# Hash attention and a SwiGLU block on one core: from the sixth pair of heads on, q and k are turned by VectorE instead of TensorE

## The chip, the cores and the metric

The kernel runs on one NeuronCore of one Trainium2 chip. The metric is the time of one execution in microseconds (us) as the device reports it. Three runs of the kernel before gave 1186.89, 1187.71 and 1187.98 us; the median is 1187.71 us. The engines are named as in the profile: PE is TensorE, PEld its weight loads, DVE is VectorE, ACT is ScalarE, POOL is GpSimd, and SP is the engine whose queue issues most of the DMAs.

## The reference, cut to what matters

```python
# q, k, v: (4 batches, 8 heads, 768 positions, 64), proj: (64, 6), all float32
q_bits = (einsum('bhsd,dk->bhsk', q, proj) > 0)          # six sign bits per position
k_bits = (einsum('bhsd,dk->bhsk', k, proj) > 0)
mask   = q_bucket[:, :, :, None] == k_bucket[:, :, None, :]   # buckets: the bits as a number
scores = where(mask, q @ k.T / 8, -1e9)
attn   = softmax(scores)                                  # with 1e-9 added to the sum
a      = attn @ v                                         # (4, 8, 768, 64)
x      = a.transpose(0, 2, 1, 3).reshape(3072, 512)
out    = (silu(x @ w_gate) * (x @ w_val)) @ w_out         # w_gate, w_val: (512, 1536), w_out: (1536, 512)
```

The three weights are float64 on the host. The kernel narrows them to float32 itself.

## The kernel before

**Pairs.** Heads are worked on in pairs, 4 pairs per batch and 16 in all, numbered 0 to 15 (the "sixth pair" is number 5). A pair has 12 units: 2 halves of the queries by 6 chunks of 128 keys. The main loop takes two units per iteration, so a pair is six iterations, called iteration 0, 2, 4, 6, 8 and 10 below after the number of their first unit in the pair (the variable `at`).

**One iteration.** Every engine works strictly in the order in which the program was written; there is no scheduler. In each iteration the program writes, in this order: `score` for two units (PE multiplies, bits first and then q and k; ACT takes the exponential into a ring of four tiles `A`), `norm` where a half of a pair is complete (PE sums into tile `sum`, DVE takes the reciprocal `r`, then `e` and `xT`), `attend` for the two units of the iteration before (PE into `av`; DVE adds the exponentials up in `acc`), and then two steps, called `mine`, of the preparation of the next pair.

**The preparation of a pair** is `front(n)`. It is written during pair n-1. Heads lie in memory as position by feature, and PE needs feature by position. So `transpose` (L205) turns three 128 by 128 blocks with the identity matrix into a PSUM tile `tps`, and ACT copies them out into `qT` or `kT` (L208). That is done for q and k and two halves, four steps. Then come four steps of `hash_bits`: one multiplication by the hash weights into `hps` (L213), followed by ACT for q (`qb`, L216) or DVE for k (`kb`, L218). The eight steps fall on iterations 2, 4, 6 and 8, two in each. For all pairs but the first, `tps`, `hps` and `sum` share one single PSUM bank (`side_bank`); each must be read out before the next can be written. Pair 0 is prepared ahead of the loop and uses the two banks of `bank` in turn.

**The second part.** When the last half of a batch is normalised (iteration 2 of pairs 4, 8 and 12, and after pair 15), `push_ffn` appends 72 "atoms" of PE work for that batch: 48 `up` atoms (results `g` and `val`, L299, in the two banks of `bank`, read out by ACT with a tanh and by DVE into `t` and `ht`) and 24 `down` atoms (`po`, L320). From then on each iteration ends with about three atoms, and the steps of `mine` stand between them. In the first batch, pairs 0 to 3, there are no atoms, and PE has only attention to do.

**DVE's extra work.** `narrow` turns the weights into float32 in 36 pieces of seven DVE instructions (L162 to L178): two or three of them in an iteration without atoms, four behind each atom, until all pieces are done. POOL fetches the pieces (`words`).

**Fetching.** `load(n+2)` is written in iteration 10 of pair n: two DMAs each for q and k (192 KB each, 256-byte runs) and one for v, all on SP's queue, where the stores of `out` stand too.

Of the kernel before, what the change touches and what calls it, by code (L numbers as in the profile page):

```python
# [8 lines left out]
FP32 = mybir.dt.float32  # L9
# [8 lines left out]
def kernel(  # L18
# [17 lines left out]
    CH = NCH // 2  # L36
    HQ = CH * P
    NP = H // 2
    DM = H * D
# [39 lines left out]

    def load(n):  # L80
        b, pr = pairs[n]
        for name, src in (("q", q), ("k", k)):
            t = raw.tile([P, NCH, 2, D], FP32, tag=name + "raw", name=name + "raw")
            for h in range(2):
                nc.sync.dma_start(t[:, :, h, :],  # L85
                                  src[b, 2 * pr + h].rearrange("(p c) d -> p c d", c=NCH))
            raws[name, n] = t
        t = raw.tile([P, 2, NCH, D], FP32, tag="vraw", name="vraw")
        nc.sync.dma_start(
            t.rearrange("p h c d -> p h (c d)"),  # L90
            v[b, 2 * pr : 2 * pr + 2].rearrange("h (p c) d -> p h (c d)", c=NCH),
        )
        raws["v", n] = t

    load(0)

    hash_w = {}  # L100
    for name in "qk":
        hash_w[name] = konst.tile([P, P], FP32, tag="hash" + name, name="hash" + name)
        nc.vector.memset(hash_w[name], 0.0)
        for o in (0, D):
            for at in (0, NBITS) if name == "q" else (0,):
                nc.sync.dma_start(hash_w[name][o : o + D, o + at : o + at + NBITS], proj[:, :])

    def column(name, first, second, third, rest):
# [11 lines left out]
    times_k = column("times_k", OFF, -OFF / 2, -NBITS * OFF / 2, 0.0)  # L120
    ident = konst.tile([P, P], FP32, tag="ident", name="ident")
    make_identity(nc, ident)
    ones = konst.tile([P, D], FP32, tag="ones", name="ones")
    nc.vector.memset(ones, 1.0)


# [66 lines left out]
    T = {}  # L193
    bits = {}

    def front(n, bank=side_bank):


        def transpose(name, half):
            if half == 0:  # L200
                T[name, n] = opnd.tile([P, S], FP32, tag=name + "T", name=name + "T")
                bits[name, n] = opnd.tile([P, S], BF16, tag=name + "b", name=name + "b")
            ps = bank("tps")
            for i in range(CH):
                nc.tensor.transpose(ps[:, i * P : (i + 1) * P],  # L205
                                    raws[name, n][:, half * CH + i, :, :].rearrange("p h d -> p (h d)"),
                                    ident)
            nc.scalar.copy(T[name, n][:, half * HQ : (half + 1) * HQ], ps[:, 0:HQ])  # L208

        def hash_bits(name, half):  # L210
            cols = slice(half * HQ, (half + 1) * HQ)
            ps = bank("hps")
            nc.tensor.matmul(ps[:, 0:HQ], hash_w[name], T[name, n][:, cols], start=True, stop=True)  # L213
# [74 lines left out]

    atoms = []

    def push_ffn(b):
# [47 lines left out]

    for step in front(0, bank):  # L340
        step()
# [75 lines left out]
```

## Time and profile before

| what | value |
|---|---|
| median of three runs | 1187.71 us |
| the profiled execution's own time | 1187.64 us |
| its span on the core | 1185.9 us |
| outside the span | 1.7 us |
| PE, DVE, ACT busy | 98%, 43%, 24% |
| preparation of pair 0, ahead of the first score | 0 to 13.25 us |
| first batch (no atoms yet) | 13.25 to 143.37 us |
| pairs 4 to 15, attention with atoms between | 143.37 to about 1010 us |
| atoms alone | from about 1010 us to the end |

The profile comes from one execution whose time is within 0.1 us of the median. In rows of the timeline, the first number is the start in us, the second the time that the row covers, then engine, line, operation and "written tile <- read tiles". A row may cover several instructions (xN); each float32 product is recorded as two matmuls. What stands in square brackets is the time for which the engine sat idle before, and what ended that. In the chain of waits a piece is "start, length, engine and line". PE work is pipelined, so the recorded lengths of neighbours overlap: what a step costs is read from start to start.

### The profile page before, as it was taken

What the parts mean: (1) busy time and instruction counts of PE and PEld (TensorE: products, weight loads), DVE (VectorE), ACT (ScalarE), POOL (GpSimd) and SP (SyncE); (2) the same over time, 40 slices, a digit from 0 to 9 for tenths busy, and PEclk for the clock granted to TensorE, in tenths of its full rate; (3) what the DMA queues carried; (4) which work ended last, traced back from release to release, by engine and by line L of the source; (5) the groups of instructions that cost most, each with busy time, mean ns of one, the idle gap of its engine ahead of it and who ended that gap; (6) DMA issues with size and microseconds to landing.
All of it is one profiled execution on the core that took longest, in us unless ns stands there. A gap on an engine that the chain in (4) does not pass through costs nothing.

```text
span 1185.9 us, 10899 instructions
## 1 busy us (share of the span) xinstructions
PE 1156.9 (98%) x4480; PEld 573.2 (48%) x4480; DVE 508.2 (43%) x756; ACT 280.3 (24%) x441; POOL 19.2 (2%) x44
## 2 busy tenths in 40 slices
PE   7888899999999999999999999999999999999998
PEld 3333355555544445555554445555554444555543
DVE  3777689998852323343331233333233222222100
ACT  4444422222212222222221213222131211000000
POOL 0000000000000000000000000000000000000000
PEclk9999999999999999999999999999999999999999
DMA  5322222324210120100002012010000000000000
GB/s 142 76 76 76 58 79 92 101 71 113 88 40 18 37 57 1 40 1 1 14 1 58 18 36 49 1 40 1 14 1 1 18 18 18 1 1 0 1 27 27
DMA packets 63698, 44.76 MB, mean 38 GB/s; under 512 B 51872, under 2 KB 55968, under 8 KB 63648
## 3 DMA queue, kind: packets, MB, share of 16 engines
q1 hardware_dynamic: 58752, 26.23, 8.6%
q0 software_dynamic: 4896, 17.83, 4.9%
q8 instruction: 35, 0.57, 0.2%
q14 instruction: 15, 0.12, 0.0%
HBM read 37.76 MB, written 6.29 MB: 37 GB/s over the span
## 4 chain that ended last, share of the span: by engine, by line
PE 97%; DVE 2%; ACT 1%; DMA 0%; SPq 0%; issue 0%; ACTq 0%
PE val L299 21%; PE g L299 21%; PE po L320 21%; PE sc L244 14%; PE av L255 11%; PE hps L213 4%; PE sum L276 2%; PE tps L205 2%; DVE r L279 2%; ACT qb L216 0%; ACT qT L208 0%; DMA kraw<-in_k_dram 0%; SPq L85 0%; ACT A L246 0%; ACT o L324 0%
## 5 line engine op out<-in xcount | busy, mean ns | idle before, releaser
L299 PE MATMUL val<-xT,wv 128*128 128x384 f32 x768 | 266.2, 489 | 0.0
L299 PE MATMUL g<-xT,wg 128*128 128x384 f32 x768 | 265.9, 489 | 0.0
L320 PE MATMUL po<-wo,ht 128*128 128x512 f32 x576 | 257.1, 597 | 0.0
L246 ACT ACTIVATE A<-sc 128x768 f32<-128x768 f32 x192 | 155.5, 812 | 208.2 <-PE sc L244 177.0
L299 PEld LDWEIGHTS val<-xT,wv 128*128 128x128 f32 x768 | 142.5, 190 | 105.4 <-DVE acc L263 6.0
L299 PEld LDWEIGHTS g<-xT,wg 128*128 128x128 f32 x768 | 142.5, 190 | 105.1 <-DVE acc L263 6.0
L320 PEld LDWEIGHTS po<-wo,ht 128*128 128x128 f32 x576 | 106.8, 190 | 134.1 <-issue 130.7
L244 PE MATMUL sc<-qT,kT 64*128 64x384 f32 x768 | 156.0, 485 | 0.0
L279 DVE RECIPROCAL r<-sum 128x384 f32<-128x384 f32 x32 | 81.8, 2556 | 151.9 <-PE sum L276 151.9
L255 PE MATMUL av<-A,vraw 128*64 128x386 f32 x768 | 144.8, 498 | 0.0
L306 DVE SCALAR_TENSOR_TENSOR t<-t,g 128x384 f32<-128x384 f32 x96 | 53.1, 554 | 206.3 <-ACT t L305 206.3
L263 DVE TENSOR_TENSOR acc<-acc,A 128x768 f32<-128x768 f32 x128 | 122.3, 955 | 35.2 <-ACT A L246 30.3
L305 ACT ACTIVATE t<-g 128x384 f32<-128x384 f32 x96 | 47.1, 490 | 351.6 <-PE g L299 347.0
L311 DVE SCALAR_TENSOR_TENSOR ht<-t,val 128x384 f32<-128x384 f32 x96 | 53.1, 553 | 125.0 <-PE val L299 125.0
L255 PEld LDWEIGHTS av<-A,vraw 128*64 128x64 f32 x768 | 49.6, 137 | 82.4 <-issue 81.3
L244 PEld LDWEIGHTS sc<-qT,kT 64*128 64x128 f32 x768 | 69.0, 190 | 21.5 <-issue 21.5
L244 PE MATMUL sc<-qb,kb 64*128 64x384 bf16 x384 | 63.8, 329 | 0.1
L218 DVE TENSOR_SCALAR kb<-hps,above_k,times_k 128x384 bf16<-128x384 f32 x32 | 21.6, 675 | 83.9 <-PE hps L213 83.4
L244 PEld LDWEIGHTS <-kb 64*128 64x128 bf16 x384 | 18.7, 93 | 67.9 <-issue 55.1
L324 ACT COPY o<-po 128x512 f32<-128x512 f32 x24 | 14.0, 585 | 144.3 <-PE po L320 142.0
L216 ACT ACTIVATE qb<-hps,nudge 128x384 bf16<-128x384 f32 x32 | 18.6, 581 | 69.4 <-PE hps L213 69.3
L213 PE MATMUL hps<-qT,hashq 128*128 128x384 f32 x64 | 27.7, 515 | 5.5 <-DVE e L281 5.5
(58 smaller groups left out, 409.9 us busy)
## 6 DMA issues: line engine op xcount, KB each, us to landing
qraw<-in_q_dram SPq DMA_DIRECT2D x32, 192.0 KB, 3.7
kraw<-in_k_dram SPq DMA_DIRECT2D x32, 192.0 KB, 4.6
vraw<-in_v_dram SPq DMA_DIRECT2D x16, 384.0 KB, 3.4
words<-in_moe_w_val_dram POOLq DMA_DIRECT2D x12, 512.0 KB, 3.8
words<-in_moe_w_out_dram POOLq DMA_DIRECT2D x12, 512.0 KB, 3.6
out_dram<-o SPq DMA_DIRECT2D x24, 256.0 KB, 2.0
words<-in_moe_w_gate_dram POOLq DMA_DIRECT2D x10, 512.0 KB, 3.9
words<-in_moe_w_gate_dram SPq DMA_DIRECT2D x2, 512.0 KB, 5.8
```

The lines of the kernel that those rows point to most:

```text
L205: nc.tensor.transpose(ps[:, i * P : (i + 1) * P], raws[name, n][:, half * CH + i, :, :].rearrange("p h d -> p (h d)"), ident)
L213: nc.tensor.matmul(ps[:, 0:HQ], hash_w[name], T[name, n][:, cols], start=True, stop=True)
L244: nc.tensor.matmul(sc[:, h, 0:HQ], x["k", n][rows, ks], x["q", n][rows, qs], start=start, stop=not start)
L246: nc.scalar.activation(ring[u % RING][:, :, 0:HQ], sc[:, :, 0:HQ], AF.Exp, scale=SCALE)
L255: nc.tensor.matmul(ps[h * D : (h + 1) * D, 0:AW], raws["v", n][:, h, c, :], a[:, h, :], start=c == 0, stop=c == NCH - 1)
L263: nc.vector.tensor_tensor(acc[n, half], acc[n, half], a[:, :, 0:HQ], op=ALU.add)
L279: nc.vector.reciprocal(r, ps[:, 0:HQ])
L299: nc.tensor.matmul(ps[:, 0:HQ], w[:, j, f * P : (f + 1) * P], x[:, j, half * HQ : (half + 1) * HQ], start=j == 0, stop=j == NJ - 1)
L305: nc.scalar.activation(t, ps[:, 0:HQ], AF.Tanh, scale=0.5)
L306: nc.vector.scalar_tensor_tensor(out=t, in0=t, scalar=1.0, in1=ps[:, 0:HQ], op0=ALU.add, op1=ALU.mult)
L311: nc.vector.scalar_tensor_tensor(out=ht, in0=now["t"], scalar=0.5, in1=ps[:, 0:HQ], op0=ALU.mult, op1=ALU.mult)
L320: nc.tensor.matmul(ps, hs[half][f][:, i * P : (i + 1) * P], wo[:, f, :], start=f == 0, stop=f == NF - 1)
```

## The change

The change has three parts.

**Turning by DVE.** For pairs 5 to 15, q and k are fetched with four DMAs each instead of two. Each of them brings 32 features of one head to 32 partitions, 96 KB in runs of 128 bytes, such that every 32 by 32 block of the tile is still position by feature but stands where its turned block belongs. One DVE instruction for q and one for k (`nc.vector.transpose`, 128 by 768 float32) then turns all blocks in place of the four PE steps and the four ACT copies. `front` of these pairs has six steps, two of DVE in iteration 2, and the four of `hash_bits` in iterations 4 and 6.

**Banks of the first batch.** `front_bank` gives a step the single side bank if atoms are waiting. If none are, every third step (counted over all such steps) gets the side bank, and the other two get the banks of the atoms. This holds for the fronts of pairs 0 to 4.

**The start.** k of pair 0 goes on ACT's queue. The hash weights are fetched once per half (two DMAs on ACT's queue instead of six on SP's) and put in place by six small DVE copies. POOL instead of DVE clears their tiles. Nine multiplications of a tile of zeros stand at the head of PE.

PE in iterations 2 and 4 of pair 4, where the first atoms stand (`tps` and `hps` belong to the front of pair 5). Before:

```order
L276 MATMUL sum<-acc,ones 64x384 x2
L255 MATMUL av<-A,vraw 64x386 x4
L299 MATMUL g<-xT,wg 128x384 x4
L205 MATMUL tps<-ident,qraw 128x128 x3
L299 MATMUL val<-xT,wv 128x384 x4
L205 MATMUL tps<-ident,kraw 128x128 x3
L299 MATMUL g<-xT,wg 128x384 x4
```

and with the change:

```order
L320 MATMUL sum<-acc,ones 64x384 x2
L299 MATMUL av<-A,vraw 64x386 x4
L341 MATMUL g<-xT,wg 128x384 x4
L341 MATMUL val<-xT,wv 128x384 x4
L341 MATMUL g<-xT,wg 128x384 x4
```

The two `tps` steps are gone from PE; the same happens in iteration 4, where now the first two `hps` steps stand.

DVE at the same place, from the reciprocal on. Before:

```order
L279 RECIPROCAL r<-sum 128x384
L281 TENSOR_SCALAR e<-avs 128x1
L282 SCALAR_TENSOR_TENSOR xT<-avs,e,r 128x384
L259 SCALAR_TENSOR_TENSOR acc<-A 128x768
L306 SCALAR_TENSOR_TENSOR t<-t,g 128x384
L176 TENSOR_SCALAR words<-words 128x512
L178 SCALAR_TENSOR_TENSOR wv<-words,wv 128x512
L162 TENSOR_SCALAR wg<-words 128x512
L165 SCALAR_TENSOR_TENSOR wg<-words,wg 128x512
L311 SCALAR_TENSOR_TENSOR ht<-t,val 128x384
L168 SCALAR_TENSOR_TENSOR wg<-words,wg 128x512
```

and with the change:

```order
L348 SCALAR_TENSOR_TENSOR t<-t,g 128x384
L203 TENSOR_SCALAR words<-words 128x512
L205 SCALAR_TENSOR_TENSOR wv<-words,wv 128x512
L189 TENSOR_SCALAR wg<-words 128x512
L192 SCALAR_TENSOR_TENSOR wg<-words,wg 128x512
L258 STREAM_TRANSPOSE qT<-qraw 128x768
L353 SCALAR_TENSOR_TENSOR ht<-t,val 128x384
L195 SCALAR_TENSOR_TENSOR wg<-words,wg 128x512
L198 TENSOR_SCALAR words<-words 128x512
L201 ISA wg<-words,wg 128x1024
L203 TENSOR_SCALAR words<-words 128x512
L258 STREAM_TRANSPOSE kT<-kraw 128x768
```

The transpose of q now stands ahead of `ht` of the second atom, that of k ahead of `t` of the third.

ACT's queue at the start, before:

```order
L208 ACT_TABLE_LOAD
L208 COPY qT<-tps 128x384
L208 COPY kT<-tps 128x384
L208 COPY qT<-tps 128x384
L208 COPY kT<-tps 128x384
```

and with the change:

```order
L100 DMA kraw<-in_k_dram 128x6x64 x2
L127 DMA proj<-in_proj_dram 64x6 x2
L241 ACT_TABLE_LOAD
L241 COPY qT<-tps 128x384
L241 COPY kT<-tps 128x384
```

Four DMA issues now stand ahead of the table load; SP loses eight there.

The diff, cut to what the prediction speaks of:

```diff
-    def load(n):
+    def load(n, k_queue=nc.sync):
         b, pr = pairs[n]
-        for name, src in (("q", q), ("k", k)):
+        for name, src, queue in (("q", q, nc.sync), ("k", k, k_queue)):
             t = raw.tile([P, NCH, 2, D], FP32, tag=name + "raw", name=name + "raw")
+            if n > NP:
+                blocks = t.rearrange("p c a b -> p (c a b)").rearrange(
+                    "p (c a d) -> p c a d", a=P // BLOCK, d=BLOCK)
+                for h in range(2):
+                    for x in range(D // BLOCK):
+                        at = h * D + x * BLOCK
+                        queue.dma_start(
+                            blocks[at : at + BLOCK],
+                            src[b, 2 * pr + h][:, x * BLOCK : (x + 1) * BLOCK].rearrange(
+                                "(a p c) d -> p c a d", c=NCH, p=BLOCK))
+                raws[name, n] = t
+                continue
...
-    load(0)
+    load(0, nc.scalar)
+
+    ident = konst.tile([P, P], FP32, tag="ident", name="ident")
+    make_identity(nc, ident)
+    zeros = konst.tile([P, 512], BF16, tag="zeros", name="zeros")
+    nc.vector.memset(zeros, 0.0)
+    for _ in range(9):
+        ps = bank("idle")
+        nc.tensor.matmul(ps, zeros[:, 0:P], zeros, start=True, stop=True)
+    two_proj = konst.tile([P, NBITS], FP32, tag="proj", name="proj")
+    for o in (0, D):
+        nc.scalar.dma_start(two_proj[o : o + D, :], proj[:, :])
     hash_w = {}
     for name in "qk":
         hash_w[name] = konst.tile([P, P], FP32, tag="hash" + name, name="hash" + name)
-        nc.vector.memset(hash_w[name], 0.0)
-        for o in (0, D):
-            for at in (0, NBITS) if name == "q" else (0,):
-                nc.sync.dma_start(hash_w[name][o : o + D, o + at : o + at + NBITS], proj[:, :])
+        nc.gpsimd.memset(hash_w[name], 0.0)
...
+    for name in "qk":
+        for o in (0, D):
+            for at in (0, NBITS) if name == "q" else (0,):
+                nc.vector.tensor_copy(hash_w[name][o : o + D, o + at : o + at + NBITS],
+                                      two_proj[o : o + D, :])
...
-    def front(n, bank=side_bank):
+    atoms = []
+    turn = iter(range(1 << 20))
+    def front_bank(name):
+        return side_bank(name) if atoms or next(turn) % 3 == 2 else bank(name)
+    def front(n):
...
-            ps = bank("tps")
+            ps = front_bank("tps")
...
-            ps = bank("hps")
+            ps = front_bank("hps")
...
+        def transpose_blocks(name):
+            T[name, n] = opnd.tile([P, S], FP32, tag=name + "T", name=name + "T")
+            nc.vector.transpose(T[name, n], raws[name, n].rearrange("p c h d -> p (c h d)"))
+
         steps = []
-        for half in range(2):
+        if n > NP:
             for name in "qk":
-                steps.append(lambda name=name, half=half: transpose(name, half))
+                steps.append(lambda name=name: transpose_blocks(name))
+        else:
+            for half in range(2):
+                for name in "qk":
+                    steps.append(lambda name=name, half=half: transpose(name, half))
...
-    for step in front(0, bank):
+    for step in front(0):
         step()
```

More of the change, by code (lines that the diff above doesn't have):

```diff
@@ L37 @@
     HQ = CH * P
+    BLOCK = 32
     NP = H // 2
@@ L78 @@
     raws = {}
-    def load(n):
+    def load(n, k_queue=nc.sync):
         b, pr = pairs[n]
-        for name, src in (("q", q), ("k", k)):
+        for name, src, queue in (("q", q, nc.sync), ("k", k, k_queue)):
             t = raw.tile([P, NCH, 2, D], FP32, tag=name + "raw", name=name + "raw")
+            if n > NP:
[10 more added lines that the diff above has]
+                continue
             for h in range(2):
-                nc.sync.dma_start(t[:, :, h, :],
+                queue.dma_start(t[:, :, h, :],
                                   src[b, 2 * pr + h].rearrange("(p c) d -> p c d", c=NCH))
@@ L120 @@
     times_k = column("times_k", OFF, -OFF / 2, -NBITS * OFF / 2, 0.0)
-    ident = konst.tile([P, P], FP32, tag="ident", name="ident")
-    make_identity(nc, ident)
     ones = konst.tile([P, D], FP32, tag="ones", name="ones")
     nc.vector.memset(ones, 1.0)
+    for name in "qk":
[3 more added lines that the diff above has]
+                                      two_proj[o : o + D, :])
     RING = 4
@@ L210, in hash_bits @@
         def hash_bits(name, half):
+            if half == 0:
+                bits[name, n] = opnd.tile([P, S], BF16, tag=name + "b", name=name + "b")
             cols = slice(half * HQ, (half + 1) * HQ)
-            ps = bank("hps")
+            ps = front_bank("hps")
             nc.tensor.matmul(ps[:, 0:HQ], hash_w[name], T[name, n][:, cols], start=True, stop=True)
@@ L286, in norm @@
             push_ffn(b)
-    atoms = []
     def push_ffn(b):
```

1 line of the change is left out of this document (removed).

## The prediction

> **What bounds the kernel now.** I read the busy shares first, then the chain of waits in three windows, then the timeline of PE inside each.
>
> ```profile
> PE 1156.9 (98%) x4480; PEld 573.2 (48%) x4480; DVE 508.2 (43%) x756; ACT 280.3 (24%) x441; POOL 19.2 (2%) x44
> by line: PE hps L213 32.7%; DMA kraw<-in_k_dram 27.5%; PE tps L205 17.6%; SPq L85 14.6%; issue 2.6%
> by line: PE sc L244 34.6%; PE av L255 20.4%; DVE r L279 13.8%; PE hps L213 11.3%; PE tps L205 6.5%; PE sum L276 5.0%; ACT qb L216 3.6%; ACT qT L208 3.0%; issue 1.1%; ACT A L246 0.6%; DVE e L281 0.2%
> by line: PE g L299 25.9%; PE val L299 25.8%; PE po L320 19.5%; PE sc L244 12.3%; PE av L255 10.2%; PE hps L213 2.9%; PE sum L276 2.0%; PE tps L205 1.5%
> ```
>
> The three chains cover 0 to 13.31 us, 13.25 to 143.37 us and 143.37 to 1120 us. In the last, the chain is PE alone: whatever leaves PE there shortens the kernel, and nothing else does. In the first batch the chain also runs through DVE (`r`) and ACT (`qb`, `qT`): PE waits there. The start is a chain of fetches and of PE work. So there are three sums.
>
> **PE turns removed from pairs 5 to 15.** Eleven fronts lose four steps each, 44 steps. The timeline of PE in pair 5 gives the price from start to start:
>
> ```profile
> 229.89 0.49 PE L205 MATMUL tps<-ident,qraw 128*128 128x128 f32 x3
> 230.21 2.75 PE L299 MATMUL g<-xT,wg 128*128 128x384 f32 x8
> 232.80 0.49 PE L205 MATMUL tps<-ident,kraw 128*128 128x128 f32 x3
> 233.12 2.75 PE L299 MATMUL val<-xT,wv 128*128 128x384 f32 x8
> ...
> 241.65 0.81 PE L213 MATMUL hps<-qT,hashq 128*128 128x384 f32 x2
> 242.30 2.74 PE L299 MATMUL val<-xT,wv 128*128 128x384 f32 x8
> ```
>
> A step costs 0.33 us (229.89 to 230.21), not the 0.49 that its records cover, and 44 of them are 14.5 us. The chain says the same: 1.5% of 976.6 us is 14.6. The `hps` steps, 0.65 us each, stay and only move two iterations forward. The 44 ACT copies that go are worth nothing: ACT is busy for 24%, under PE.
>
> **What DVE takes over.** No row shows a 32 by 32 transpose, so I bound it. DVE's times for plain instructions, a group's row each (last number before the idle time: mean ns of one):
>
> ```profile
> L162 DVE TENSOR_SCALAR wo<-words 128x512 int32<-128x512 int32 x12 | 5.0, 421 | 0.0
> L263 DVE TENSOR_TENSOR acc<-acc,A 128x768 f32<-128x768 f32 x128 | 122.3, 955 | 35.2 <-ACT A L246 30.3
> L279 DVE RECIPROCAL r<-sum 128x384 f32<-128x384 f32 x32 | 81.8, 2556 | 151.9 <-PE sum L276 151.9
> ```
>
> At the rate of the first, 768 columns take 0.63 us; at that of the reciprocal 5.1 us; the `acc` addition has exactly this shape and takes 0.955. I take 0.955: a transpose moves every float32 once, with no division. Two per pair are 1.9 us. From about 345 us on, `narrow` is done and DVE mostly idles, so they lie under PE. Until then, in pairs 4, 5 and 6, DVE is nearly full. Here are a window of iteration 2 in pair 5 (DVE busy 11.72 of 12.01), what DVE waited for from 143 to 335 us, and the two rows next to the new instructions:
>
> ```profile
> 211.62:223.63 12.01, 11.72 (x20) 1.00 0.30 89
> ...
> DVE t L306 <- ACT t L305: 13.3, 18, 1.7
> DVE ht L311 <- PE val L299: 3.2, 5, 0.9
> ...
> 224.66 0.55 DVE L306 SCALAR_TENSOR_TENSOR t<-t,g 128x384 f32<-128x384 f32 x1 [0.25 <-ACT t L305]
> ...
> 230.09 0.55 DVE L311 SCALAR_TENSOR_TENSOR ht<-t,val 128x384 f32<-128x384 f32 x1 [0.49 <-PE val L299]
> ```
>
> 16.5 us of waiting in 192 us is 6.2 per pair of 72; the transposes take 1.9 of it and the shorter PE time 1.3 (4 by 0.33). So the room suffices in sum. Locally, `t` done at 225.2 frees the bank that the `g` of 230.21 writes, with 5 us to spare; `ht` done at 230.64 frees that of the `val` of 233.12, with 2.5. That second one becomes late first: DVE comes 1.9 later, less the 0.25 and 0.49 that it idled, and PE two steps earlier in each of two iterations, 1.3 us, so 2.5 - 1.2 - 1.3 leaves nothing. I put 0.1 to 0.2 us of PE stall on each of three pairs, 0.4 in all; with 2 us per transpose it would be 2.2 us per pair. This part gives 14.5 - 0.4 = 14.1 us.
>
> **The fetch.** Its runs halve to 128 bytes, so q and k are 6144 packets instead of 3072. The shortest way from issue to use is where SP's queue is held by stores:
>
> ```profile
> 411.10 1.29 SPq L85 DMA_DIRECT2D qraw<-in_q_dram  x2
> ...
> 411.00:419.00 8.00, 8.00 (x28) 3.38 (x25) 1.92 (x2) 1.63 (x2) 0.00 (x0) 1.00 0.54 132
> ...
> 433.48 0.49 PE L205 MATMUL tps<-ident,qraw 128*128 128x128 f32 x3
> ```
>
> The window (second number from the end: the share of the DMA engines) holds this fetch alone: 0.54 of 8 us, 4.3 us. Halved runs cost between that (if bytes decide) and 8.6 us (if packets do); eight issues at 0.65 take 5.2. I take 8.6, landed by about 421, 12 us ahead of 433. SP issues four more DMAs per pair, 2.6 us, ahead of the next `v` and stores, which wait for PE and ACT in any case. I cost it at nothing; without that cover it would cost what it is late, in front of everything on DVE.
>
> **Three banks in the first batch.** In the chain, a pair of `tps` steps and one of `hps` steps look like this:
>
> ```profile
> 23.14 0.49 PE tps L205 x3
> ...
> 23.66 0.49 ACT qT L208
> ...
> 24.19 0.55 PE tps L205 x3
> 24.74 1.72 PE sc L244 x12
> ...
> 27.91 0.86 PE hps L213 x2
> ...
> 28.79 0.59 ACT qb L216
> ...
> 29.42 0.91 PE hps L213 x2
> 30.33 1.72 PE sc L244 x12
> ```
>
> The second step waits until ACT has emptied the one bank. With another bank it follows at once: 1.60 us become 2 by 0.33, and 2.42 become 2 by 0.65. There are eight of each in fronts 1 to 4: 8 x 0.94 + 8 x 1.12 = 16.5 us. The bank is also shared with `sum`, and the steps behind a `norm` wait for the reciprocal. PE's waits from 13 to 143 us:
>
> ```profile
> PE hps L213 <- DVE e L281: 5.5, 4, 1.4
> PE hps L213 <- ACT qb L216: 5.4, 8, 0.7
> PE tps L205 <- ACT qT L208: 4.6, 8, 0.6
> PE tps L205 <- DVE e L281: 4.1, 3, 1.4
> ```
>
> Seven waits for `e`, 1.37 us each. Counting every third step onto the side bank, step 14 (front 1), 32 and 38 (front 4) still stand there as the first behind a `norm` and wait as before; 17 and 23 (front 2) stand second, and the wait shrinks by the 0.33 and 0.65 of the step ahead; front 3 has none there. That saves 1.0 + 2.7 = 3.7, together 20.2 us. DVE is the limit on it:
>
> ```profile
> 72.39:103.60 31.21, 23.83 (x32) 1.00 0.27 72
> ```
>
> A pair that hosts front 3 falls from 31.2 to 24.4 us while DVE needs 23.8 in it. DVE then has no slack behind its reciprocals, the next `sum` waits for `acc`, and I take 1.0 off: 19.2 us.
>
> **The start.**
>
> ```profile
> 4.20 2.43 SPq L106 DMA_DIRECT2D hashq<-in_proj_dram  x4
> ...
> 4.79 0.87 PE L205 MATMUL tps<-ident,qraw 128*128 128x128 f32 x3 [4.79 <-DMA qraw<-in_q_dram]
> ...
> 13.25 0.34 PE L244 MATMUL sc<-qb,kb 64*128 64x384 bf16 x2
> ...
> 16.78 0.43 DVE L162 TENSOR_SCALAR wg<-words 128x512 int32<-128x512 int32 x1 [2.76 <-DMA words<-in_moe_w_gate_dram]
> ...
> L244 PE MATMUL sc<-qb,kb 64*128 64x384 bf16 x384 | 63.8, 329 | 0.1
> ```
>
> q lands at 4.8 as before; k is issued 1.4 us earlier. The first `tps` (0.87 for three, later 0.49) and `hps` steps run at half rate because PE has just begun; the nine multiplications of zeros fill the wait for q. By the last row (329 ns for 384 columns in bf16), nine of 512 columns are 3.9 us at most at full rate, from about 1.1 to 5.0, so they hold q up by 0.2 us or not at all. Hash weights: issued behind k at about 2.1 to 3.3, landed 3 us later, copied by 6.8. Four `hps` at 0.65 end at 9.4 instead of 13.25: 3.8 us. If the rate is still halved then, they take 5.2 and 1.2 us is left. The Trainium skill ("TensorE: Matmul & The Clock Gate", Part 1) says that about 3.4 us of sustained work release the clock; by that the zeros suffice and 3.8 holds. The trace here shows only that rate doubles between 4.8 and about 11.4 us. DVE cannot go on before the first weights land (16.78), which now can come at most 3.6 us earlier; the third exponentials wait on DVE's `acc`, for which I take 0.5 off: 3.3 us.
>
> **The sum.** 14.1 + 19.2 + 3.3 = 36.6 us off the profiled execution's 1187.64 us (0.07 below the median, span 1185.9): 1151 us.
>
> **A rule on the clock.** The profile's granted clock fell once:
>
> ```profile
> 114.00:116.00 2.00, 2.00 (x10) 0.55 0.36 39
> ```
>
> The same work took 1.6 us longer there (clock 0.55 and 0.59 for 4 us, after a stretch of waits and transposes). The same page (Part 4) says that transposes do not count as activity for the clock; by that, fewer waits make this dip less likely, and the sum would be 1149.4. I keep it in, since waits remain; two such dips would be 1152.6.
>
> **Rivals.**
> (A) As summed, with its own range of 1145 to 1157: 0.62.
> (B) The first batch is held by DVE. If pairs 1 to 3 take 27.5 us each (23.8 of DVE plus the waits for `sum` and `e` that stay) instead of some 25, 8 us are lost: 1159. For it speaks how near 23.8 is to 24.4; against it that it is still below, and that fronts 1, 2 and 4 leave their pairs longer. 0.20.
> (C) The transposes take 2 us or more, and pairs 4 to 6 stall by 2 to 3 us each: 1157 to 1160. 0.08.
> (D) The fetch is late where stores hold it. Were a packet three times as dear, 26 us, q would be late by 4 us at three places, with DVE's queue stuck behind it: 1163 to 1166. Against it: 12 us of room. 0.05.
> (E) Slower than before: the transpose runs at the reciprocal's rate, 5.1 us. It stands ahead of `ht` and `t`, so the `t` of the third atom comes 10.2 us late with 5 to spare: some 4 to 6 us of PE stall in each of eleven pairs, 50 us, against 36.6 + 0.4 gained: 1200. It decides from about 2.6 us per transpose on, where stalls begin in all pairs, and outweighs the gain from about 4.5. 0.04.
> (F) The change doesn't do what it says: banks still clash and DVE's copy of the weights holds the start, so that only the 14 us come: 1173. 0.01.
>
> **How the numbers follow.** The time is A's, 1151. The range reaches down to 1143: A without the dip (1.6), without the 1.9 us that I took off for DVE, and with 4 us more if the start and the waits for `e` go wholly; and up over B, C and D to 1167. What a measurement can tell from no change is about 0.2%, 2.4 us: A, B, C, D and F are faster, of which 0.01 goes to the same for E's weaker forms: 0.95, 0.01 and 0.04.
>
> **What would show it.** Right: `tps` left only up to about 110 us, first score near 9.5 us, the first atom near 120 instead of 143.37, pair 5 lasting about 1.3 us less, transposes near 1 us, PE without waits from then on. Wrong: transposes above 2 us, PE waiting for `t` or `ht` in pairs 4 to 6, DVE waiting for `qraw`, a first score after 11 us, or more waits for `e` and `acc` before the first atom.

## The result, and the profile after

The changed kernel takes 1154.18 us (median of four runs, 1154.02 to 1154.55) against 1187.3 us (four runs, 1186.25 to 1187.98): a ratio of 0.9722, with a 95% interval of 0.9705 to 0.9739. It is 33 us faster; 1151 was predicted, in a range of 1143 to 1167. The profiled execution took 1154.3 us, its span is 1152.5.

The profile of the changed kernel opens with the busy shares; the chain of waits follows for the first batch (12.7 to 123.5 us) and for what lies behind it (to 1000 us):

```profile
PE 1139.5 (99%) x4357; PEld 562.2 (49%) x4357; DVE 527.4 (46%) x783; ACT 260.9 (23%) x397; POOL 19.5 (2%) x46
...
by line: PE sc L288 39.7%; PE av L299 25.7%; DVE r L323 11.5%; PE hps L248 10.6%; PE sum L320 5.9%; PE tps L238 5.6%; ACT A L290 0.7%; issue 0.3%; DVE e L325 0.2%
by line: PE g L341 23.9%; PE val L341 23.6%; PE po L362 21.7%; PE sc L288 13.7%; PE av L299 11.4%; PE hps L248 3.2%; PE sum L320 2.2%; DVE wv L205 0.1%; DVE t L348 0.1%; ACT t L347 0.1%; DVE words L203 0.0%; issue 0.0%
```

PE loses 17 us of busy time. Its wait for the reciprocal (`r`) has become shorter but is still in the chain of the first batch; `qb` and `qT` of ACT are gone from it. Behind the first atom, `tps` is gone and nothing has come in its place: DVE has 0.2% of that chain.

Where the time went is read from two marks in the timeline of PE, the first score and the first atom. After:

```profile
12.72 0.34 PE L288 MATMUL sc<-qb,kb 64*128 64x384 bf16 x2
...
123.55 2.85 PE L341 MATMUL g<-xT,wg 128*128 128x384 f32 x8
```

Before, these stood at 13.25 and 143.37, and the span ended at 1185.9. The same two marks were read in every run below, and all the stretches of this document come from them:

| kernel | first score | first score to first atom | first atom to the end | median us (runs) |
|---|---|---|---|---|
| before | 13.25 | 130.12 | 1042.53 | 1187.3 (4) |
| after | 12.72 | 110.83 | 1028.95 | 1154.18 (4) |
| predicted off | 3.3 | 19.2 | 14.1 | 36.6 |
| found off | 0.5 | 19.3 | 13.6 | 33.1 |
| DVE turns alone | 13.56 | 130.10 | 1028.54 | 1172.89 (4) |
| three banks alone | 12.51 | 110.82 | 1042.47 | 1168.29 (4) |
| after, old start | 11.90 | 110.82 | 1028.6 | 1153.81 (4) |
| after, k of pair 0 behind q (a single run) | 10.81 | 110.83 | 1028.3 | 1151.73 (1) |
| the same, four runs | 12.89 | 110.82 | 1028.3 | 1151.96 (4) |
| after, 14 multiplications of zeros | 11.36 | 110.83 | 1029.1 | 1153.11 (1) |
| after, each DVE turn twice | 12.36 | 110.82 | 1030.5 | 1155.67 (4) |
| after, runs of 64 bytes | 11.24 | 110.84 | 1029.0 | 1154.35 (4) |
| after, DVE turns from pair 2 on | 11.33 | 108.57 | 1028.5 | 1151.1 (4) |
| after, two banks | 13.48 | 105.06 | 1029.0 | 1149.19 (4) |
| after, two banks, k behind q | 13.13 | 105.06 | 1028.3 | 1148.0 (5) |

The stretches of a row come from its profiled execution, and the last column is the median, so they do not add up to it exactly: the three stretches found are 33.4 us in all, the medians 33.1 us apart. Among runs with the same banks and the same turns in the first batch, the middle column repeats within 0.02 us. The left one moves by 1.5 to 2.1 us also between runs whose start is the same; the section on the start says why. The right one lies within 0.9 us for all kernels with DVE turns (the doubled turn apart), and that spread has its place: it stands behind the last multiplication. These are the last rows of PE, before and after:

```profile
1164.49 17.76 PE L320 MATMUL po<-wo,ht 128*128 128x512 f32 x41
```

```profile
1137.78 10.46 PE L362 MATMUL po<-wo,ht 128*128 128x512 f32 x24
```

They end at 1182.25 and 1148.24. From the first atom to the end of the last multiplication it is 1038.9 us before and 1024.7 after, 14.2 us less, and it is 1024.7 in every other run with single DVE turns as well. Behind it comes only the copy and the store of the last rows of `out`, which take 3.7 us before and 4.3 after.

### The profile page after: what moved, and what is told of

Its sections match the earlier page's. It is cut to its first block, busy times and chain, and to the rows that moved or that the text cites. A ratio compares the mean times of both kernels' runs of the same rounds, so it can differ in the third digit from the quotient of the medians.

```text
span 1152.5 us, 10719 instructions
## 1 busy us (share of the span) xinstructions
PE 1139.5 (99%) x4357; PEld 562.2 (49%) x4357; DVE 527.4 (46%) x783; ACT 260.9 (23%) x397; POOL 19.5 (2%) x46
## 4 chain that ended last, share of the span: by engine, by line
PE 98%; DVE 1%; DMA 0%; ACT 0%; SPq 0%; issue 0%; ACTq 0%
PE g L341 22%; PE po L362 22%; PE val L341 22%; PE sc L288 14%; PE av L299 11%; PE hps L248 4%; PE sum L320 2%; DVE r L323 1%; PE tps L238 1%; DMA qraw<-in_q_dram 0%; ACT A L290 0%; DVE wv L205 0%; SPq L100 0%; ACT o L366 0%; DVE t L348 0%
## 5 line engine op out<-in xcount | busy, mean ns | idle before, releaser
L366 ACT COPY o<-po 128x512 f32<-128x512 f32 x24 | 14.1, 586 | 159.7 <-PE po L362 159.7
L303 DVE SCALAR_TENSOR_TENSOR acc<-A 128x768 f32<-128x768 f32 x32 | 30.5, 952 | 0.5 <-ACT A L290 0.5
```

The source lines that it names most:

```text
L303: nc.vector.scalar_tensor_tensor(out=acc[n, half], in0=ring[(u - 1) % RING][:, :, 0:HQ], scalar=S * EPS / P, in1=a[:, :, 0:HQ], op0=ALU.ad ...
```

## The turns on DVE, alone and doubled

**DVE turns alone.** Start and banks stay as in the kernel before; only pairs 5 to 15 are turned by DVE:

```diff
-    load(0, nc.scalar)
+    load(0)
 ... (the start as before: six DMAs of hash weights on SP's queue, no zeros)
-        return side_bank(name) if atoms or next(turn) % 3 == 2 else bank(name)
+        return side_bank(name) if next(turn) >= 8 else bank(name)
```

> Turning by VectorE alone: start and banks as before (side bank for every front but the first). Theory (what leaves TensorE behind the first atom is the gain, 44 steps of 0.33 us less about 0.6 to 0.9 lost): 13.6 us faster, ratio about 0.9885, first atom at 143.4 us as before, and from there to the end 1029 us instead of 1042.5. Rival (the 13.6 us behind the first atom hang on the earlier start of that stretch, or part of it comes from the banks): under 10 us.

Measured: 1172.89 us, ratio 0.9874 (0.9857 to 0.989). The time is won behind the first atom (14.0 us, 14.2 to the last multiplication) and nowhere else. The instructions themselves, from the groups of the changed kernel (busy us, mean ns, idle time of DVE before them):

```profile
L258 DVE STREAM_TRANSPOSE qT<-qraw 128x768 f32<-128x768 f32 x11 | 10.7, 970 | 0.0
L258 DVE STREAM_TRANSPOSE kT<-kraw 128x768 f32<-128x768 f32 x11 | 10.6, 965 | 0.0
```

0.97 us each, 1 to 2% above the addition of the same shape that the prediction took; and DVE never waits for the fetched tile. With that, the rivals of a slow transpose fall.

**Each turn twice.** The second copy writes the same values again, so it only doubles DVE's load:

```diff
-            nc.vector.transpose(T[name, n], raws[name, n]...)
+            for _ in range(2):
+                nc.vector.transpose(T[name, n], raws[name, n]...)
```

> The changed kernel with each transpose of VectorE issued twice into the same tile (11 pairs, 0.97 us more each for q and k; the result is unchanged). Theory of the prediction (no room is left between ht and the val that takes its bank in pairs 4 to 6, while behind 345 us VectorE has room): 1 to 2 us of stall on each of pairs 4 to 6, 3 to 6 us in all, seen as TensorE waiting for t or ht there, and nothing in pairs 7 to 14. Rival (the 9.3 us for which VectorE still waits between 120 and 340 us cover it): within 1 us of the changed kernel's 1154.2.

Measured: 1155.67 us (1155.32 to 1155.82), 1.5 us above the changed kernel, between the two answers that were expected; 0.9734 (0.9717 to 0.975). By the prediction's local margin 2 us per turn should have cost 2.2 us in each of three pairs, and 0.97 us should have left nothing at the `val` that waits for the bank of `ht`. That place in the changed kernel (iteration 4 of pair 5), PE and then DVE:

```profile
208.42 0.81 PE L248 MATMUL hps<-qT,hashq 128*128 128x384 f32 x2
209.06 2.74 PE L341 MATMUL g<-xT,wg 128*128 128x384 f32 x8
211.64 0.81 PE L248 MATMUL hps<-kT,hashk 128*128 128x384 f32 x2
212.29 2.74 PE L341 MATMUL val<-xT,wv 128*128 128x384 f32 x8
```

```profile
210.08 0.55 DVE L353 SCALAR_TENSOR_TENSOR ht<-t,val 128x384 f32<-128x384 f32 x1
```

`ht` ends at 210.63 and `val` starts at 212.29: 1.7 us of room, not none. The step that was wrong is in these rows: the prediction let PE come 1.3 us sooner, two steps less in each of two iterations. But the two `hps` steps now stand where two `tps` steps had stood. They take 0.64 each (208.42 to 209.06) instead of 0.33, and so give back what the two steps missing in iteration 2 had won. PE does not come sooner here: counted from the `sum` of iteration 2 (213.34 before, 192.53 after), this `val` starts after 19.8 us in both kernels. `ht` ends after 17.3 us before and after 18.1 now, so of the 2.5 us of room go only the 0.8 by which DVE is later, and 1.7 are left. With the turns doubled, 1.94 us more stand against 1.66 of room, and the same place shows the difference:

```profile
211.75 0.55 DVE L354 SCALAR_TENSOR_TENSOR ht<-t,val 128x384 f32<-128x384 f32 x1
```

```profile
212.35 2.85 PE L342 MATMUL val<-xT,wv 128*128 128x384 f32 x8 [0.27 <-DVE ht L354]
```

Over the run, PE's waits for `ht` and `t` are 0.3 and 0.4 us. From the first atom to the end of the last multiplication it takes 1.2 us longer (1025.9 against 1024.7); the other 0.5 of that is not put down to any wait in the profile. Most of the added work went into time in which DVE had waited for ACT: from 119 to 345 us, in the changed kernel and then with the turns doubled,

```profile
DVE t L348 <- ACT t L347: 8.2, 11, 1.5
```

```profile
DVE t L349 <- ACT t L348: 3.9, 6, 1.4
```

**From pair 2 on.** If DVE takes the turns at 0.97 us each, why not earlier?

```diff
-            if n > NP:
+            if n > 1:
 ... (the same in front)
```

> The changed kernel, but VectorE turns q and k from pair 2 on instead of pair 5. Theory with VectorE as the bound of the first batch: a pair there needs 23.8 + 1.9 = 25.7 us of VectorE, so the three pairs that prepare pairs 2, 3 and 4 cannot fall below 25.7 us (now 26.7, 24.9 and 27.7), TensorE waits for acc or the reciprocal in new places, and the first atom comes 2 us earlier at most (121.5 or later). Rival (VectorE has room): 6 steps pairs of 0.8 us and two or three waits of 1 us go, first atom 7 to 8 us earlier, near 116.

Measured: 1151.1 us (1150.3 to 1153.36); 0.9695 (0.9681 to 0.971). In the first batch PE loses the twelve turns of fronts 2 to 4 (six pairs of steps at 0.81, 4.9 us, as the section on the banks shows) and most of its waits for `e` (5.5 to 1.4). Of these 9.0 us, 2.3 come out. Two equal windows of the first batch, and PE's waits in the run:

```profile
60.00:85.00 25.00, 22.78 (x134) 9.71 (x134) 24.28 (x33) 11.65 (x16) 1.06 (x2) 1.00 0.39 81
85.00:110.00 25.00, 23.05 (x134) 9.52 (x130) 24.38 (x33) 11.65 (x16) 0.53 (x1) 1.00 0.35 78
```

```profile
PE sc L288 <- ACT A L290: 3.4, 3, 1.2
PE hps L248 <- DVE qT L258: 2.0, 3, 0.7
...
PE hps L248 <- DVE e L325: 1.4, 1, 1.4
```

DVE (the third busy figure) is at 24.3 of 25.0 us. PE waits for `qT` (2.0 us) and for the exponentials (`A`, 3.4 us). Behind one of the latter stands DVE too: ACT had sat idle for 4.7 us for DVE's `acc` before it could begin (at 60.31), and PE then waited 1.1 us for ACT (at 61.18). So this edit brings about the rival in which DVE holds the first batch: two turns, 1.9 us more of DVE work in a pair, are enough for it. The changed kernel, which leaves these turns on PE, stays short of it.

## The banks of the first batch

**Three banks alone**, with the start and the turns of the kernel before:

```diff
-            if n > NP:
+            if n > 99:
 ... (the same in front, and the start as before)
```

> The three banks alone: start as before, all pairs turned by TensorE. Theory: the first batch (first score to first atom) takes 110.8 us instead of 130.1 where no dip of the clock occurs, 19.3 us faster (17.7 by steps and waits, 1.6 by the dip), and nothing changes behind the first atom (1042.5 us). Rival (the dip at 114 us was made by the transposes and stays, since all transposes are still on TensorE): 17.7 us, with a granted clock below 0.9 in some window before the first atom.

Measured: 1168.29 us (1167.6 to 1168.4); 0.9836 (0.9821 to 0.985). The first batch is 19.3 us shorter, as in the changed kernel, and the rest is as before. So the whole middle column belongs to the banks. The chain of the changed kernel in that stretch:

```profile
17.86 0.81 PE tps L238 x6
...
25.81 1.49 PE hps L248 x4
...
29.86 2.56 DVE r L323
...
32.47 1.56 PE hps L248 x4
```

A pair of `tps` steps takes 0.81 us instead of 1.60, one of `hps` 1.49 instead of 2.42: 8 x 0.79 + 8 x 0.93 = 13.8 us. The second step of each no longer waits for ACT. The waits of PE that are left:

```profile
PE hps L248 <- DVE e L325: 3.2, 3, 1.4
PE tps L238 <- DVE e L325: 2.3, 2, 1.4
...
PE val L341 <- DVE wv L205: 0.3, 1, 0.3
```

5 waits for `e` and 5.5 us remain of 7 and 9.6: 4.1 us gone. They fall on steps 14, 17, 23, 32 and 38, the five that the prediction had counted. The stretch of halved clock at 114 to 118 us is not there (1.6 us), although every turn still stands on PE. Together 13.8 + 4.1 + 1.6 = 19.5, against 19.3 found.

**Two banks.** If a step on the side bank waits for `e` because it shares the bank with `sum`, then the third bank is what keeps those 5.5 us:

```diff
-        return side_bank(name) if atoms or next(turn) % 3 == 2 else bank(name)
+        return side_bank(name) if atoms else bank(name)
```

> The changed kernel, but while no atoms wait every step of the fronts takes one of the two banks of the atoms and none the side bank. Theory (the remaining waits of TensorE for the reciprocal, 3.2 + 2.3 us in five places, come only from steps on the side bank): these waits go to zero and the first atom comes 5.5 us earlier, at 118 us; 1148.7 us. Rival (VectorE is the limit by then, 23.8 us per pair): the waits move to the sums (for acc), and less than 3 us are gained.

Measured: 1149.19 us (1148.6 to 1149.62); 0.9676 (0.9661 to 0.969), 5.0 us below the changed kernel, although its start was 0.8 us later. The first batch takes 105.06 us, 5.8 less. A window inside it, and the only wait of PE in the batch that the profile of this run shows:

```profile
62.00:86.00 24.00, 23.79 (x143) 10.56 (x140) 22.48 (x31) 12.95 (x20) 1.05 (x2) 1.00 0.34 94
```

```profile
PE sum L320 <- DVE acc L307: 0.2, 1, 0.2
```

Every wait for `e` is gone, and none for ACT has come back in the batch (one of 0.2 us stands ahead of the first score): two banks in turn are enough, since two steps stand next to each other and the next two follow some 4 us later. DVE has 22.5 of 24 us to do: it is near, but PE sets the pace.

## The fetch

Runs of 64 bytes and eight DMAs per tensor, that is, the price of the new layout once more doubled:

```diff
-                        queue.dma_start(blocks[at : at + BLOCK], ...)
+                        for y in range(0, BLOCK, 16):
+                            queue.dma_start(blocks[at : at + BLOCK, :, :, y : y + 16], ...)
```

> The changed kernel with the fetches of q and k of pairs 5 to 15 cut into runs of 64 bytes, eight DMAs for each instead of four. Theory (the fetch lies under other work with 12 us of room at the tightest place): 12288 packets and 16 issues of 0.65 us take up to 17 us, still landed before the transposes; within 1 us of 1154.2, no wait of VectorE for qraw or kraw. Rival (the fetch is near its limit): VectorE waits for qraw in pairs 8, 11 and 12, 3 us or more in all.

Measured: 1154.35 us (1152.93 to 1155.39); 0.9723 (0.9708 to 0.9737), the same as the changed kernel. SP's queue at the place that the prediction looked at, first in the changed kernel, then with 64 bytes:

```profile
386.37 2.75 SPq L93 DMA_DIRECT2D qraw<-in_q_dram  x4
389.22 2.71 SPq L93 DMA_DIRECT2D kraw<-in_k_dram  x4
...
409.91 0.97 DVE L258 STREAM_TRANSPOSE qT<-qraw 128x768 f32<-128x768 f32 x1
```

```profile
384.91 5.56 SPq L94 DMA_DIRECT2D qraw<-in_q_dram  x8
...
408.44 0.97 DVE L259 STREAM_TRANSPOSE qT<-qraw 128x768 f32<-128x768 f32 x1
```

The first issue stands 23.5 us ahead of the use in both, and DVE has no wait for `qraw` or `kraw` in either run. The changed kernel's page gives 3.4 us from issue to landing:

```profile
qraw<-in_q_dram SPq DMA_DIRECT2D x44, 96.0 KB, 3.4
```

With the last of the four issued at about 389, q has landed by about 392.5, 17 us before it is used. The cover is larger than the 12 us that were reckoned.

## The start

**Without the new start.** Everything else as in the changed kernel:

```diff
-    load(0, nc.scalar)
+    load(0)
 ... (six DMAs of hash weights on SP's queue, DVE clears their tiles, no zeros)
```

> The change without its start (k on SP, six DMAs of hash weights on SP, no zeros). By the prediction the start is worth 3.3 us: 1157.5. If k on ACT's queue takes back what the early hash weights and the zeros bring (first score 12.7 in the profile of the change against 12.5 to 13.6 of the old start), it is worth nothing: 1153.5 to 1155, with the first score between 12.5 and 13.6 and the first atom about 110.8 us later.

Measured: 1153.81 us (1153.16 to 1154.16); 0.9717 (0.9703 to 0.973), against 1154.18 (1154.02 to 1154.55) with it. The 3.3 us of the prediction are not there at all; the new start is worth nothing that these runs can tell. PE's timeline in the profile of the changed kernel:

```profile
1.19 4.02 PE L120 MATMUL idle<-zeros 128*128 128x512 bf16 x9 [1.19 <-DVE nudge L134]
6.91 0.87 PE L238 MATMUL tps<-ident,qraw 128*128 128x128 f32 x3 [1.70 <-DMA qraw<-in_q_dram]
...
9.49 1.37 PE L248 MATMUL hps<-qT,hashq 128*128 128x384 f32 x2
10.69 0.81 PE L248 MATMUL hps<-kT,hashk 128*128 128x384 f32 x2
```

q lands at 6.9 us, not 4.8: the `tps` of q waits 1.7 us behind the zeros. Then the turns and the first `hps` run at half rate (0.87 and 1.37 instead of 0.52 and 0.81). This is read from their durations: the column of the granted clock shows 1.00 from 6.8 to 10.2 us all the same. The two DMAs of q among the issues of the first 3 us (the last number: median us from issue to landing), in the changed kernel and then in the one before:

```profile
qraw<-in_q_dram SPq DMA_DIRECT2D x2, 192.0 KB, 4.7
```

```profile
qraw<-in_q_dram SPq DMA_DIRECT2D x2, 192.0 KB, 3.2
```

With k on its way at the same time, q takes longer to land.

**k behind q on SP's queue**, with the rest of the new start kept:

```diff
-    load(0, nc.scalar)
+    load(0)
```

A single run:

> The changed kernel with k of pair 0 back on the queue of q, behind it. Theory (q came at 6.8 us instead of 4.8 because k, issued at the same time on another queue, shares the DMA engines with it): q lands near 4.8 again, k near 6.6, the first product of q starts near 5.2 and the first score about as early as now, 12 to 13 us. Rival (q is late for another reason, such as v close behind it): q still lands after 6 us.

and four runs more:

> The change with k of pair 0 behind q on SP, and nothing else. If the shared DMA engines are what makes q late (6.8 instead of 4.8 us), q is back near 4.8, PE has no gap behind the zeros, the first score stands near 10.8 and the time is 1151.5 to 1152.5. If the place of k does not matter and only the time at which PE reaches its full rate does, which varies from one execution to the next, the time is 1153.5 to 1154.5 in the median.

Measured: 1151.73 us in the single run, then 1151.96 us (1151.76 to 1153.79); 0.9705 (0.9692 to 0.9718). By the medians, putting k back is worth 2.2 us, and with it the rest of the new start 1.9 against the old one. The 95% intervals of the three ratios overlap; what speaks for a gain is that four of the five runs lie below every run of the changed kernel and of the old start, by at least 1.1 us. In the single run:

```profile
5.22 0.52 PE L238 MATMUL tps<-ident,qraw 128*128 128x128 f32 x3
6.92 0.52 PE L238 MATMUL tps<-ident,kraw 128*128 128x128 f32 x3 [1.18 <-DMA kraw<-in_k_dram]
...
10.81 0.34 PE L288 MATMUL sc<-qb,kb 64*128 64x384 bf16 x2
```

q is there when the zeros end (3.5 us from issue to landing), and k at 6.9. With k on ACT's queue it was q that came at 6.9: the two together are not there sooner in either order. That is why even here the first score is at 10.8 and not at the 9.4 of the prediction, whose sum had no term for the later of the two; in the kernel before, the first turn of k stands at 6.6 us. The edit also moves v and the next pair's q back by 1.3 us on SP's queue, so what k alone does to q is not told apart from that.

Of the 2.2 us, the order itself explains about half a microsecond: profiles with k on ACT's queue, three banks and PE at full rate from the first turn have their first score at 11.24 to 11.36. Another 0.7 us (1028.3 against 1029.0 behind the first atom) stands behind the last multiplication: the last store takes 2.0 us from issue to landing in the profile of the four runs and 2.7 in the changed kernel. From the end of PE to the end of the span it is 3.6 to 3.9 us in the seven profiles with k on SP's queue and 3.8 to 4.6 in the six with k on ACT's; why is open. The rest, about 1 us, is put down to how often PE is at half rate at the start, which only the profiled executions show.

**More zeros.** Fourteen multiplications instead of nine, so that PE has no gap before q:

```diff
-    for _ in range(9):
+    for _ in range(14):
```

> The changed kernel with 14 instead of 9 multiplications of zeros ahead, so that TensorE works without a gap from 1.2 to about 7.2 us. Theory (nine, 4.0 us, and then a gap of 1.7 us do not hold a whole window of the clock's monitor, so the turns and the first hash product of pair 0 run at half rate, and a gapless stretch releases it): the turns start at 0.4 us from each other instead of 0.64, the hash products at 0.65, and the first score comes near 11.4 us. Rival (products of zeros do not count): half rate until about 10.7 us as now, first score at 12.7 to 13.2.

Measured: 1153.11 us in a single run, the first score at 11.36.

```profile
1.19 5.77 PE L120 MATMUL idle<-zeros 128*128 128x512 bf16 x14 [1.19 <-DVE nudge L134]
7.00 0.52 PE L238 MATMUL tps<-ident,qraw 128*128 128x128 f32 x3
```

Nine take 4.02 us and fourteen 5.77: 0.45 us each at first and 0.35 for the last five. The rate rose within them, and the turns run at full rate from the first. One run does not show that this always happens, nor that it needs the five more: with nine zeros and the same start, two profiles have the first turn at 0.87 or 0.88 us (the changed kernel, the doubled turns: first score 12.72 and 12.36) and three at 0.52 (64-byte runs and turns from pair 2 on: 11.24 and 11.33; two banks, where the clock was halved again from 8.5 us on: 13.48).

## Both findings together

Two banks and k behind q:

> Two banks instead of three in the first batch, and k of pair 0 fetched on SP behind q. If the two gains stand on different stretches (5.0 us between the first score and the first atom, 1.9 to 2.4 us before the first score), they add: 1154.2 - 5.0 - 2.2 = about 1147 us, first score near 10.8 and first atom near 116 us. If DVE holds the first batch once the waits for e are gone (its work begins only when the first weight words land, not with the first score), the earlier start is given back there: about 1149 us, first atom at 118.5 us as with two banks alone.

Measured: 1148.0 us (five runs, 1146.88 to 1148.29) against 1187.64 (nine runs); 0.9664 (0.9651 to 0.9677). The time lies between the two answers. The first batch takes 105.06 us again, but the profiled execution hardly tests whether DVE gives an earlier start back, since its first score, at 13.13, is only 0.35 us earlier than with two banks alone; that two of the five runs are at 1146.9 speaks against it. That the median lies 1.2 and not 2.2 us below the two banks alone is the start again: the other three runs are at 1148.0 to 1148.3, and the profiled one, 1148.29, had its clock halved after it had been released. Besides, the edit of the banks also takes the third bank from the front of pair 0. In this profile a turn of k waits 0.24 us for ACT's `kT` there, and the last `hps` follows the one before it after 0.96 us (11.32 to 12.28) instead of 0.64 (11.34 to 11.98 in the changed kernel). So the two gains do not stand on wholly different stretches. Windows (the third number from the end is the granted clock) of the two runs with k behind q that show this, then of the two banks alone:

```profile
4.55:7.95 3.40, 1.76 (x11) 0.95 (x9) 0.43 (x4) 0.90 (x3) 0.00 (x0) 1.00 1.16 272
7.95:11.35 3.40, 3.29 (x8) 1.98 (x9) 0.00 (x0) 1.50 (x4) 0.00 (x0) 0.50 1.27 242
```

```profile
4.90:8.30 3.40, 1.49 (x11) 1.12 (x11) 0.05 (x1) 0.71 (x2) 0.00 (x0) 0.99 1.09 264
8.30:11.70 3.40, 3.40 (x9) 2.13 (x8) 0.11 (x1) 1.69 (x4) 0.00 (x0) 0.50 1.18 231
```

```profile
5.10:8.50 3.40, 1.65 (x13) 1.26 (x12) 0.64 (x6) 0.97 (x3) 0.00 (x0) 1.00 1.23 262
8.50:11.90 3.40, 3.28 (x8) 1.69 (x6) 0.17 (x1) 1.43 (x3) 0.00 (x0) 0.50 1.22 280
```

The second pair is the run of k behind q that took 1153.79, 1.8 to 2.0 us more than the three others; its first score is 2.08 us later than in the single run of the same kernel.

## Why the prediction was right, and where not

**PE turns removed: right, 14.1 against 14.2 to the last multiplication** (13.6 to the end of the span, whose last store took longer in that profile). 44 steps at 0.33 are 14.5, less a wait of 0.3. The transposes took 0.97 us, 0.955 was taken. The stall of 0.4 us at the bank of `ht` was not found, because PE does not come sooner there: "PE two steps earlier in each of two iterations" overlooked that `hps` steps take the place of the second two. The only wait of PE behind the first atom in the changed kernel is the 0.3 us, at another place, for the narrowed weight `wv`; the run with the old banks and start shows the same one, and the two kernels without turns on DVE do not have it. That it is about as long as the expected stall is luck.

**The fetch at nothing: right.** With runs halved once more it still costs nothing.

**The banks: 19.2 against 19.3, but the sum is another one.** The slots of `tps` and `hps` pairs are 0.81 and 1.49 us, and the steps had been taken as 0.66 and 1.30: 13.8 instead of 16.5. The 0.33 and 0.65 had been read between atoms; in the first batch a pair takes 0.15 and 0.19 us longer than twice that. Why was not tried. The waits for `e` gave 4.1 instead of 3.7, at the five steps that were named. Two choices made up for the difference: the 1.0 us taken off for DVE did not come, and the halved clock, which had been kept in, was gone (1.6 us). So a good part of the agreement is compensation, that is, luck.

**The start: wrong, 3.3 against 0.5 in the profile and nothing in the median.** The step that failed is "q lands at 4.8 as before". With k on ACT's queue q landed at 6.9. With that undone, 1.9 us appear by the medians, not 3.3, since then k is the one that is there at 6.9, and the sum had no term for it. The bound for the rate ("if the rate is still halved then") was the right worry: in the profile of the changed kernel PE was at half rate until about 10.6 us, zeros or not. The nine zeros took the 3.9 us reckoned for them (4.0), but not at the full rate at which that was reckoned: in the run with fourteen, the last five take 0.35 us each. The Trainium skill ("TensorE: Matmul & The Clock Gate", Part 1) was read for the 3.4 us alone; the same part says that the window runs free of the kernel and that the point of release varies by run. The traces agree with that: with nine zeros (4.0 us) and k on ACT's queue the first turn was at full rate in three profiles and at half rate in two.

**Rivals.** (B), the batch held by DVE, did not come, though its number came half-way: pairs 1 to 3 took 26.8, 24.9 and 27.8 us, between the "some 25" of (A) and the 27.5 of (B). The surplus is mostly the waits for `e`: with two banks and the same DVE work none of them is left, and the three pairs take 24.9, 25.2 and 24.9. The run with turns from pair 2 on shows how far off (B) was: less than 2 us of DVE work per pair. (C), (D), (E) and (F) did not come.

**What would show it.** The first score (near 9.5) and the first atom (near 120) were missed by 3.2 and 3.5 us, nearly all from the start; a first score after 11 us had been named as a sign of error, and it was one, for that term. The other signs hold.

**The halved clock.** The prediction weighed the rule of the Trainium skill ("TensorE: Matmul & The Clock Gate", Part 4) that transposes do not count as activity. The dip did vanish, as that rule leaned. But the turns alone, with the old banks, have a dip at another place. Windows of that run, and then the same for the kernel before:

```profile
128.40:131.80 3.40, 1.69 (x4) 0.60 (x4) 2.48 (x4) 0.58 (x1) 0.00 (x0) 0.97 0.00 0
131.80:135.20 3.40, 3.40 (x13) 1.45 (x12) 2.95 (x5) 0.81 (x1) 0.53 (x1) 0.52 0.08 20
```

```profile
110.80:114.20 3.40, 1.68 (x12) 1.08 (x14) 3.35 (x6) 0.96 (x2) 0.00 (x0) 1.00 0.61 123
114.20:117.60 3.40, 3.40 (x15) 1.21 (x12) 3.26 (x6) 1.62 (x2) 0.53 (x1) 0.50 0.53 149
```

In the stretch ahead of the dip in the first run stand only two pairs of `hps` products and the waits for `e` and `qb`, no transpose. So a dip does not need transposes; and the three banks alone, which keep every turn on PE, have none. What the two dips have in common is a PE that was busy for 1.7 of the 3.4 us ahead. But such a stretch is not always followed by one. In the kernel before, seven places of the first batch hold only 1.36 to 1.47 us of PE work in some 3.4 us, and the clock fell behind one of them. This is one of the two idlest (the clock, third number from the end, is 1.00 here and also in the 3.4 us behind it):

```profile
65.30:68.70 3.40, 1.36 (x5) 0.59 (x4) 2.87 (x4) 0.58 (x1) 0.00 (x0) 1.00 0.36 143
```

In the turns alone the same seven places recur, and the clock fell behind another one. One reading fits both: if the batch is counted off in fixed steps of 3.4 us from the start of the fall (114.25 and 131.66), the step just ahead of it is the idlest in both runs, with about 1.7 and 1.6 us of PE work, and the next idlest, with about 2.0 and 1.8, has no fall behind it. With three banks the wait for ACT behind a wait for `e` (0.6 us behind 1.4) is gone: the idlest 3.4 us of the first batch then hold 2.03 us of PE work wherever they begin, and none of the runs with new banks shows a dip behind its first score. That the idle time in such fixed steps is the cause is argued from these rows, after the fact; no run varied it alone.

## What to carry to other kernels

Before a transfer is moved to a second queue to have it earlier, ask what it will share the DMA engines with: here q came two microseconds later, and the two together no sooner. When buffers are added to a rotation, look at what else uses each of them: the third bank was shared with `sum` and kept 5.5 us of waits that two unshared banks do not have. A sum that comes out right is checked term by term: marks in the timeline that split the run into stretches showed one term missing and two that cancelled.

## What the runs showed of the hardware that was not expected

- **The clock falls for 3.4 us at a time.** In all five stretches above the granted clock is 0.50 for 3.4 us (0.52 in the row whose window is cut a little beside it), and in the 3.4 us ahead PE had been busy for 1.49 to 1.76 us. The Trainium skill ("TensorE: Matmul & The Clock Gate", Part 1) states a window of this length; the traces agree. It tells of a return to half rate after an idle window; here no gap of PE was longer than 1.9 us (the wait for k in the run of 1153.79), and the clock fell all the same.
- **The start of the same kernel differs by 2 us from run to run,** by where the release falls and whether the clock is halved again: k behind q has its first score at 10.81 in one profile and at 12.89 in another, and its times, 1151.73 and 1153.79, differ by 2.06 us. A comparison of starts needs several runs, and the marks behind the start.
- **Runs of 64 bytes** where there is time: twice the DMAs, each with half the bytes, 5.6 us of issue per tensor instead of 2.8, and no effect on the end.
